# Two linear-attention and MLP layers in split precision: another order for the scaling, turning, norms, biases and last splits beside the MLP

## The chip, the cores and the metric

One core of a Trainium2 chip runs the whole program. The metric is device time in microseconds (us), the median of several runs. The core has five queues that work in order and side by side: TensorE (PE, with its weight loads as PEld), VectorE (DVE), ScalarE (ACT), GpSimd (POOL) and SyncE (SP), which here issues nearly all transfers between the core's memory and DRAM. An instruction that waits holds up all that is behind it in its own queue.

## The reference

x has 2048 tokens of 448 values; there are 16 heads of 28. Two layers, each

```
x = x + attention(layernorm(x))        # linear attention
x = x + gelu(layernorm(x) @ w1 + b1) @ w2 + b2      # 448 -> 1792 -> 448
```

with, for each head, phi(t) = where(t > 0, t + 1, exp(t)) + 1e-6:

```
kv  = sum_s phi(k_s) v_s^T ;  z = sum_s phi(k_s)
out = (phi(q) @ kv) / (phi(q) . z + 1e-6), joined over the heads, @ wo
```

Both layers use the same weights. LayerNorm has no scale or offset. All is float32.

## The kernel before

**Precision.** Each operand of a large matmul is split into a high part, which ACT makes by a cast to a rounded format, and a low part, the rest, which DVE (for weights POOL) makes by a subtraction. A product is then high by high, high by low and low by high, summed in PSUM. So every tile costs one ACT cast and one DVE subtraction before PE can use all of it.

**Stages of a layer.** The tokens are 16 tiles of 128 and four *groups* of four tiles (the code's b or k, 0 to 3); the 1792 inner values are 14 *chunks* of 128 (i, 0 to 13).

1. `phase1` (L797 on): for each tile LayerNorm, the K product, phi(K), and the sum G of x^T phi(K) over all tiles; Q products in between, phi(Q) to DRAM (`pq_d`).
2. A transition, written out token by token in `ORDER` (L733): G becomes the small matrix M (values, mask and wo in one, with parts `Mh`, `Ml`), and group 0 goes through attention. The rest of the Q products fills PE.
3. `classic` (L1326), twice: the MLP of group 0, then of group 1. Each step i issues the first product of the next chunk (`mlp1`, L1190: `hp`, 11 matmuls of 512 columns, then gelu and split), then `behind` (the attention of groups 1 to 3), then the second product (`mlp2`, L1210: `y`, 12 matmuls of 448 columns). In step 13 of group 0 the `mlp1` issued is the first of group 1.
4. `eight` (L1382), seven times: the MLP of groups 2 and 3 together, two chunks at a time by seven products (`hx`, `hy`, `hz`) of sums of inputs instead of eight.
5. `rest` (L1478): the second MLP product of group 3, with the beginning of the next layer in between, by the list `REST` (L1476).

**Turning.** PE needs inputs with the inner dimension on the partitions. For most tiles that is done without PE: DVE turns blocks of 32x32 (`turn`, L313, into tiles `sq`), SP stores the squares to DRAM (`store_sq`, L320) and loads them back rearranged (`spread`, L325, into tiles `sp`), and ACT and DVE split what came (`split_t`, L354: cast at L364, subtraction at L365). Two tiles share one 512 KB store and load.

**The list around the change.** `PLAN` (L1253) has one string for each of the 28 steps of the two `classic` passes, here called chunks 0 to 27; 0 to 13 lie beside group 0. `behind` issues its tokens in order, loads (tokens that begin with l) first. A token is a name, a group and a tile:

- `ld`: load phi(Q); `z` (L943): POOL multiplies it by the key sums; `p` (`q_prep`, L1064): DVE sums that to denominators, scales (L962 to L973) and turns; `sq`, `lq`: store and load of the squares (second digit: pair of tiles); `q`: the split into `qh`, `ql`.
- `o`: the attention product `op` on PE (`oc_mm`, L1014), then `o_ln` (L1027): DVE adds it to x (L1033), ACT forms mean and square sum, POOL the root `brs` (L1038), and SP stores x to DRAM (`r_d`).
- `n` (`m_prep`, L1072): ACT normalises (L1054), DVE turns; `sx`, `lx`: store and load; `x` (L351): the split into the MLP's input, `XH` and `XL`.
- `g`: load x; `r`: load x from `r_d`; `b` (L1057): POOL adds the bias of the MLP's output; `s`, `t`: the sums of inputs for `eight` (POOL and DVE) and their splits.

All four tiles of a group must have gone through `x` before the group's first `hp`. Weights for coming chunks are split in steps of a generator (`make`, L484; for `eight` the longer `sevens`, L445) by ACT, POOL and DVE.

Of the kernel before, what the change touches and what calls it, by code (L numbers as in the profile page):

```python
# [22 lines left out]
def linear_attn_mlp_kernel(  # L23
# [13 lines left out]
    x0 = x_in[0]  # L37
# [4 lines left out]
    NT = S // 128  # L42
# [667 lines left out]
    def stage_g(l, t, acc, mid=lambda: None):  # L710
# [21 lines left out]

    ORDER = [  # L733
# [3 lines left out]
    ] * LAYERS  # L737
    DEFER = NT - sum(tok in ("Q", "Qa", "Qy") for tok in ORDER[0].split())
# [58 lines left out]
    def phase1(l, tr):  # L797
        za = consts.tile([128, D], F32, name="za", tag="za")
        acc = []
        load_to(l, 4 if l == 0 else NORM[l][1][-1])  # L800
        if l == 0:
            launch(za)
            load_to(l, NORM[l][2][-1])
        for t in range(l == 0, NT):
            norm = NORM[l][t] if t < len(NORM[l]) else ()
            for tok in STEPS.get((l, t), STEP).split():
                if tok[1:].isdigit() and tok[0] in "anv":
                    {"a": stage_a, "n": stage_n, "v": stage_t}[tok[0]](l, int(tok[1:]))
                elif tok == "q1":
                    stage_qphi(1)  # L810
                elif tok == "sp":
                    for key, h in list(stored):
                        block(key)
                        spread(key, h)
                elif tok == "ld" and t + 2 < len(NORM[l]):
                    load_to(l, NORM[l][t + 2][-1])
                elif tok == "a":
                    for u in norm:
                        stage_a(l, u)
                elif tok == "n":  # L820
                    for u in norm:
                        stage_n(l, u)
                elif tok == "tu":
                    for u in norm:
                        stage_t(l, u)
                elif tok == "T" and t + 1 < NT:
                    stage_b(l, t + 1, "acc" if t == 1 else "h")
                elif tok == "X" and t + 1 < NT and (l == 0 or t >= 1):
                    stage_x(l, t + 1)
                elif tok == "K":  # L830
                    stage_k(l, t)
                elif tok == "qp":
                    stage_qphi()
                elif tok == "kp":
                    stage_kphi(l, t)
                elif tok == "kh":
                    stage_kh(l, t)
                    if l == 0:
                        begin(BG[t])
                elif tok == "kl":  # L840
                    stage_kl(l, t, za)
                elif tok == "s":
                    stage_s(l, t)
                elif tok == "G" and t >= 1:
                    acc = acc or [bank("acc", 4, f"G{c}")[:, :D] for c in range(4)]
                    stage_g(l, t - 1, acc)
                elif tok == "bg" and l == 0:
                    background(BG[t - 1])
                elif tok == "Q" and t < DEFER:
                    stage_q(l, t)  # L850
            if t == 12:
                tr.wv = stage_square(wqkv[:, 2 * D:])
            if t == 13:
                trans_load(l, tr)
        return za, acc
# [354 lines left out]
    def mlp2(l, b, i, then=lambda: None):  # L1210
# [46 lines left out]
        "p13 sq11 z20 g10 ld22",  # L1257
        "q10 lq11 p20 z21 g11 ld23",
        "q11 o10 p21 sq20 z22 g12",
        "q12 o11 n10 p22 z23 g13 ld30",  # L1260
        "q13 o12 n11 sx10 ld31",
        "o13 n12 lq20 p23 sq21 z30 ld32",
        "n13 lx10 sx11 p30 z31 g20 ld33",
        "x10 lq21 p31 sq30 z32",
        "lx11 q20 x11 p32 z33 g21",
        "q21 x12 x13 o20 g22",
        "q22 o21 n20 lq30 g23",
        "q23 o22 p33 n21 sq31 sx20 g30",
        "q30 o23 n22 g31",
        "q31 lq31 o30 n23 sx21 g32",  # L1270
        "q32 o31 n30 g33",
        "q33 o32 n31 sx30 lx21 r10",
        "o33 n32 lx20 tA111 r11",
        "n33 sx31 lx30 tA121 r12 b10",
        "lx31 tA110 r13 b11",
        "sS10 sS11 tA120 b12",
        "tS10 tS11 sS30 sS20 b13",
        "sS40 tS20 sS31 sS21",
        "tS21 sS41",
        "tS40 tS41",  # L1280
# [45 lines left out]
    def classic(l, b, tr):  # L1326

        if b == 0:
            mlp1(l, 0, 0)
            moves = trans_chunks(tr)  # L1330
        for i in range(NF):
            if i + 1 < NF:
                mlp1(l, b, i + 1)
            elif b == 0:
                mlp1(l, 1, 0)
            if b == 0:
                next(moves, None)
            n = first_pair(l, b) + i // 2 + 2
            late = b and i >= NF - 4
            if late:  # L1340
                make(first_pair(l, 2))
            elif i % 2:
                make(n)
            if i % 2 == 0 and (b == 0 or i < NF - 2):
                make(n + 1)
            behind(l, b * NF + i, tr)
            if b == 0 and 9 <= i < 13:
                add_bias(l, 0, i - 9)
            if b == 0 or i < NF - 2:
                mlp2(l, b, i)  # L1350
            if b == 0:
                next(moves, None)
            if late:
                make(first_pair(l, 2))
            elif i % 2 == 0:
                make(n)
            if b and i == NF - 1:
                make(n)

    def beside(l, k):  # L1360
# [21 lines left out]
    def eight(l, k):  # L1382

        n = first_pair(l, 2) + k
        c = Pair(l, k, n)
        onward = k == NP - 1 and l + 1 < LAYERS

        def step():
            if k < NP - 1:
                make(n + 1)  # L1390

        c.product(1)
        s1 = c.keep(c.X, "s1")
        if k:
            step()
            c.product(5)
            s5 = c.keep(c.Y, "s5")
            step()
            if onward:
                stage_a(l + 1, 0)  # L1400
            c.product(2)
            dve.tensor_tensor(s1, s1, c.Z, op=OP.add)
            c.high(s1, 0)
            step()
            c.product(6)
            s2 = c.keep(c.X, "s2")
            make(n)
            if k < NP - 2:
                make(n + 2)
            step()  # L1410
            mlp2(l, 2, 2 * k - 1)
            c.low(0)
            step()
            c.product(3)
            dve.tensor_tensor(s2, s2, c.Y, op=OP.add)  # L1415
            c.high(s2, 1)
            step()
            c.product(7)
            dve.tensor_tensor(s5, c.X, s5, op=OP.add)
            c.low(1)  # L1420
            c.later(s5, 1)
            step()
            beside(l, k)
            if onward:
                stage_a(l + 1, 1)
        else:
            mlp2(l, 1, NF - 2)
            c.product(2)
            dve.tensor_tensor(s1, s1, c.Z, op=OP.add)
            token_piece(l, "A22", 0)  # L1430
            c.high(s1, 0)
            make(n + 2)
            step()
            c.product(5)
            s5 = c.keep(c.Y, "s5")
            step()
            c.product(6)
            s2 = c.keep(c.X, "s2")
            c.low(0)
            mlp2(l, 1, NF - 1)  # L1440
            step()
            c.product(7)
            dve.tensor_tensor(s5, c.X, s5, op=OP.add)
            c.later(s5, 1)
            token_piece(l, "A22", 1)
            make(n)
            step()
            c.product(3)
            dve.tensor_tensor(s2, s2, c.Y, op=OP.add)
            c.high(s2, 1)  # L1450
            c.low(1)
            step()
        mlp2(l, 2, 2 * k)
        c.product(4)
        c.later(c.X, 0)
        step()
        if k == 0:
            step()
# [14 lines left out]

    gb = Came()

    REST = ("", "n0", "n1", "a2 m0", "s0 n2", "a3 m1", "n3", "p0 m0", "s1 a4 m0", "n4", "m1", "p1 x0", "x1 m1", "")  # L1476

    def rest(l):  # L1478

# [61 lines left out]
    for l in range(LAYERS):  # L1541
# [11 lines left out]
        def ahead_pq(j):  # L1553
# [12 lines left out]
            tq=lambda j: q_transpose(l, 0, j), qh=lambda j: q_high(l, 0, j), ql=lambda j: q_low(l, 0, j), o=lambda j: o_mm(l, 0, j, tr),  # L1566
            la=lambda j: o_ln(l, 0, j), lb=lambda j: o_n(l, 0, j), x=lambda j: m_part(l, 0, j), tu=lambda j: turn_xm(l, j),
            st=lambda j: store_sq(("m", l, 0), j), sp=lambda j: spread(("m", l, 0), j),
            sa=lambda j: spread(("m", l, 0), j), pl=ahead_pq, pre=lambda j: make(first_pair(l, 0) + 2), b=biases)
        for tok in ORDER[l].split():  # L1570
            name, j = tok.rstrip("0123456789"), int("0" + tok.lstrip("abcdefghijklmnopqrstuvwxyzQTG"))
            getattr(tok_, name)(j)
        assert not fill and not qo
        table(AF.Gelu_apprx_tanh)
        q_z(l, 1, 0, tr)
        for b in range(2):
            classic(l, b, tr)
        for k in range(NP):
# [30 lines left out]
```

## Time and profile before

| | us |
|---|---|
| median of three runs | 860.82 (860.04 to 862.4) |
| the profiled execution | 860.47 |
| its span, first to last instruction | 858.8 |
| PE busy | 847.9 (99%) |
| DVE, ACT, POOL busy | 576.5, 507.2, 388.6 |

The profile is of one execution. Its timeline gives start and duration of each instruction, by engine, source line and tile, and in brackets how long the engine stood idle before it and for whose result; where an x-count is above 1, neighbours alike are merged. The view of waits sums the same idle times by who waited for whom: us in total, times, longest. The windows view gives busy time of PE, PEld, DVE, ACT and POOL in a stretch, each with its count, then the granted TensorE clock as a share of full speed, the share of busy DMA time and GB/s. The chain of waits is the work that ended last, followed back in time. The source view of one line gives shortest, median and longest duration in ns.

### The profile page before, as it was taken

The page shows a single profiled execution, that of the slowest core. Times are in us where ns is not written, and L with a number is a line of the kernel's source. Part 1 is how long each engine was busy: PE and PEld are TensorE (multiplying, and loading weights), DVE is VectorE, ACT ScalarE, POOL GpSimd, SP SyncE. Part 2 cuts the span into 40 slices and gives each one's busy share as a digit, 9 for nine tenths or more (in the row PEclk, how much of TensorE's full clock was granted, in tenths as well). Part 3 has the DMA queues.
Part 4 walks back from the last instruction along what each step waited for, and adds up shares of the span by engine and source line. Part 5 has one row for each costly group of instructions (what it writes and reads, how often), then busy time and mean ns, then how long its engine had stood idle before and what let it go on. Part 6 is the DMA issues. An engine that isn't in the chain of part 4 may idle for free.

```text
span 858.8 us, 12486 instructions
## 1 busy us (share of the span) xinstructions
PE 847.9 (99%) x4085; PEld 755.5 (88%) x4085; DVE 576.5 (67%) x1022; ACT 507.2 (59%) x1051; POOL 388.6 (45%) x460
## 2 busy tenths in 40 slices
PE   9999999999999999999999999999999999999998
PEld 8899988887888888889989998988878888888897
DVE  7899597858643765456779976867776358545443
ACT  7667665465677576664446665555656766666531
POOL 3456524537335844750533343134563357454320
PEclk9999999999999999999999999999999999999999
DMA  5375746757567134437644543477576560333261
GB/s 172 121 249 178 241 138 197 244 180 251 181 208 236 35 119 126 142 96 245 219 151 160 181 141 118 142 229 241 161 241 221 189 197 25 105 109 98 91 233 44
DMA packets 103637, 142.92 MB, mean 166 GB/s; under 512 B 9876, under 2 KB 90644, under 8 KB 103572
## 3 DMA queue, kind: packets, MB, share of 16 engines
q1 hardware_dynamic: 101156, 138.77, 49.4%
q10 hardware_dynamic: 2416, 3.36, 1.2%
q8 instruction: 32, 0.52, 0.3%
q14 instruction: 33, 0.27, 0.1%
HBM read 88.94 MB, written 49.02 MB: 161 GB/s over the span
## 4 chain that ended last, share of the span: by engine, by line
PE 78%; DVE 9%; ACT 5%; issue 4%; POOL 2%; DMA 2%; SPq 0%; DVEq 0%; POOLq 0%; ACTq 0%
PE hp L1205 12%; PE y L1236 8%; PE y L1235 8%; PE y L1237 8%; PE hx L1147 8%; PE G L724 7%; PE psk L382 6%; PE psq L382 5%; PE hy L1147 4%; PE hz L1147 2%; DMA sp<-sq_m 1%; PE op L1023 1%; PE op L1022 1%; PE op L1021 1%; DVE pq L973 1%
## 5 line engine op out<-in xcount | busy, mean ns | idle before, releaser
L1236 PE MATMUL y<-w2l,gh 128*128 128x448 f32 x447 | 164.1, 367 | 0.0
L1235 PE MATMUL y<-w2h,gh 128*128 128x448 f32 x447 | 162.5, 364 | 0.1
L1237 PE MATMUL y<-w2h,gl 128*128 128x448 f32 x447 | 160.8, 360 | 0.0
L1205 PE MATMUL hp<-XH,W 128*128 128x512 f32 x392 | 123.4, 389 | 0.0
L1182 DVE TENSOR_TENSOR gl<-g,gh 128x512 fp32r<-128x512 f32 x84 | 69.2, 823 | 71.9 <-ACT gh L1178 71.7
L1235 PEld LDWEIGHTS y<-w2h,gh 128*128 128x128 f32 x447 | 83.9, 188 | 9.8 <-DVE x L1240 0.4
L1236 PEld LDWEIGHTS y<-w2l,gh 128*128 128x128 f32 x447 | 84.0, 188 | 6.8
L1237 PEld LDWEIGHTS y<-w2h,gl 128*128 128x128 f32 x447 | 84.0, 188 | 5.4
L1205 PE MATMUL hp<-XL,W 128*128 128x512 f32 x224 | 85.5, 390 | 1.6 <-DVE XL L365 1.6
L1205 PEld LDWEIGHTS hp<-XH,W 128*128 128x128 f32 x392 | 73.5, 188 | 12.9 <-ACT XH L364 0.3
L1159 ACT ACTIVATE g<-s,b1s 128x256 f32<-128x256 f32 x84 | 38.2, 502 | 55.0 <-DVE s L1415 34.9
L1038 POOL TENSOR_TENSOR brs<-bst,few 128x1 f32<-128x1 f32 x32 | 18.0, 564 | 105.6 <-ACT bst L1036 94.4
L1207 ACT ACTIVATE g<-hp,b1s 128x512 f32<-128x512 f32 x56 | 38.4, 685 | 42.5 <-PE hp L1205 39.9
L382 PE MATMUL psk<-wk,XH 128*128 128x448 f32 x210 | 61.8, 364 | 0.0
L563 POOL TENSOR_TENSOR xnl<-x,xnh 128x384 fp32r<-128x384 f32 x32 | 35.0, 1093 | 53.6 <-ACT xnh L562 30.6
L382 PE MATMUL psq<-wq,XH 128*128 128x448 f32 x196 | 57.2, 366 | 0.3 <-DVE eq L401 0.3
L425 POOL TENSOR_TENSOR W<-temp,W 128x256 fp32r<-128x256 f32 x56 | 48.1, 879 | 20.5 <-ACT W L424 20.5
L309 DVE STREAM_TRANSPOSE sq<-xm 128x384 f32<-128x384 f32 x32 | 20.7, 647 | 50.1 <-ACT xm L1054 49.9
L1178 ACT CAST gh<-g 128x512 fp32r<-128x512 f32 x84 | 52.2, 621 | 2.7
L1205 PEld LDWEIGHTS hp<-XL,W 128*128 128x128 f32 x224 | 41.9, 188 | 11.1 <-DVE XL L365 2.4
L951 POOL TENSOR_TENSOR pz<-pq,zb 128x448 f32<-128x448 f32 x24 | 29.1, 1214 | 45.8 <-DVE dn L962 45.8
L213 POOL TENSOR_TENSOR brs<-bve,few 128x1 f32<-128x1 f32 x31 | 17.1, 551 | 69.1 <-DVE bve L212 63.6
(252 smaller groups left out, 2162.1 us busy)
## 6 DMA issues: line engine op xcount, KB each, us to landing
temp<-in_B_w_dram SPq DMA_DIRECT2D x28, 384.0 KB
x<-in_A_x_dram SPq DMA_DIRECT2D x32, 224.0 KB
pq_d<-eq SPq DMA_DIRECT2D x32, 224.0 KB
pq<-pq_d SPq DMA_DIRECT2D x32, 224.0 KB
g_d<-g SPq DMA_DIRECT2D x28, 256.0 KB
x<-x_d SPq DMA_DIRECT2D x32, 224.0 KB
gb<-g_d SPq DMA_DIRECT2D x28, 256.0 KB
sq_a<-sq SPq DMA_DIRECT2D x13, 512.0 KB
```

What stands on the lines that cost most here:

```text
L382: pe.matmul(o, x, p, start=(i == 0), stop=(i == 10))
L425: pool.tensor_tensor(lo, x, f(hi), op=OP.subtract)
L724: pe.matmul(acc[c], w, k, start=first and c not in others[0], stop=last and c not in others[1])
L1147: pe.matmul(o, w, r, start=(k in (1, 5, 2) and i == 0), stop=(i == len(made) - 1), skip_group_check=True)
L1159: act.activation(g[:, s].rearrange("p (u i n) -> p i u n", u=2, i=4), x[:, s].rearrange("p (i u n) -> p i u n", u=2, i=4), AF.Gelu_apprx_t ...
L1178: act.copy(gh, g)
L1182: dve.tensor_sub(gl, g, f(gh))
L1205: pe.matmul(hp, w, r, start=(k == 0), stop=(k == len(made) - 1))
L1207: act.activation(g, hp, AF.Gelu_apprx_tanh, bias=b1s[:, i:i + 1])
L1235: pe.matmul(acc[j], gh[:, s], hi, start=first, stop=False)
L1236: pe.matmul(acc[j], gh[:, s], lo, start=False, stop=False)
L1237: pe.matmul(acc[j], gl[:, s], hi, start=False, stop=stop)
```

## The change

In `PLAN`:

- Norms `n` of groups 1 to 3 stand ahead of the next tile's sum `o` instead of behind it (chunks 6 to 8 and 13 to 19).
- `x10` goes from chunk 10 to chunk 11, behind `q20`. `p32` and `z33` go from chunk 11 to chunk 12, behind `x12 x13 o20`. The store `sq30` goes from chunk 10 to chunk 11, where the load `lx11` is issued ahead of it.
- The loads `r10` to `r13` go from chunks 18 to 21 to chunks 17 and 18, and the biases `b10` to `b13` from chunks 20 to 23 to 19 to 22.

In `classic`: the four biases of group 0 go from steps 9 to 12 to steps 5 to 8; the weight step that stood at the end of group 1's last step is issued in `eight` instead, behind the first product and its copy `s1`. In `ORDER`: `z10` is issued by a new token `z1` behind the third tile's statistics, instead of at the end of the list. At the seam of the layers: the splits x2 and x3 of layer 1's first group are done in the last step of `rest` instead of in `phase1`, with the store s1 a step earlier and the load p1 a step earlier (chunk 10 instead of 11).

```diff
-        "ms2 m3 ms3 ql0 Qy Qi tq2 qh2 pl1 pl0 pl2 qs3 o1 la1 ql2 o0 tq3 qh3 Qj Qs la0 lb1 ql3 tu1 st1 o2 la2 lb0 tu0 st0 sp1 o3 la3 lb2 tu2 st2 sp0 "
+        "ms2 m3 ms3 ql0 Qy Qi tq2 qh2 pl1 pl0 pl2 qs3 o1 la1 ql2 o0 tq3 qh3 Qj Qs la0 lb1 ql3 tu1 st1 o2 la2 lb0 z1 tu0 st0 sp1 o3 la3 lb2 tu2 st2 sp0 "
...
-                elif tok == "X" and t + 1 < NT and (l == 0 or t >= 1):
+                elif tok == "X" and t + 1 < NT and (l == 0 or t >= 3):
                     stage_x(l, t + 1)
...
         "q11 o10 p21 sq20 z22 g12",
-        "q12 o11 n10 p22 z23 g13 ld30",
-        "q13 o12 n11 sx10 ld31",
-        "o13 n12 lq20 p23 sq21 z30 ld32",
+        "q12 n10 o11 p22 z23 g13 ld30",
+        "q13 n11 o12 sx10 ld31",
+        "n12 o13 lq20 p23 sq21 z30 ld32",
         "n13 lx10 sx11 p30 z31 g20 ld33",
-        "x10 lq21 p31 sq30 z32",
-        "lx11 q20 x11 p32 z33 g21",
-        "q21 x12 x13 o20 g22",
-        "q22 o21 n20 lq30 g23",
-        "q23 o22 p33 n21 sq31 sx20 g30",
-        "q30 o23 n22 g31",
-        "q31 lq31 o30 n23 sx21 g32",
-        "q32 o31 n30 g33",
-        "q33 o32 n31 sx30 lx21 r10",
-        "o33 n32 lx20 tA111 r11",
-        "n33 sx31 lx30 tA121 r12 b10",
-        "lx31 tA110 r13 b11",
-        "sS10 sS11 tA120 b12",
-        "tS10 tS11 sS30 sS20 b13",
+        "lq21 p31 z32",
+        "lx11 q20 x10 x11 sq30 g21",
+        "q21 x12 x13 o20 p32 z33 g22",
+        "q22 n20 o21 lq30 g23",
+        "q23 n21 o22 p33 sq31 sx20 g30",
+        "q30 n22 o23 g31",
+        "q31 lq31 n23 o30 sx21 g32",
+        "q32 n30 o31 g33 r10 r11",
+        "q33 n31 o32 sx30 lx21 r12 r13",
+        "n32 o33 lx20 tA111 b10",
+        "n33 sx31 lx30 tA121 b11",
+        "lx31 tA110 b12",
+        "sS10 sS11 tA120 b13",
+        "tS10 tS11 sS30 sS20",
...
-            if b == 0 and 9 <= i < 13:
-                add_bias(l, 0, i - 9)
+            if b == 0 and 5 <= i < 9:
+                add_bias(l, 0, i - 5)
...
-            if b and i == NF - 1:
-                make(n)
...
         else:
+            step()
             mlp2(l, 1, NF - 2)
...
-    REST = ("", "n0", "n1", "a2 m0", "s0 n2", "a3 m1", "n3", "p0 m0", "s1 a4 m0", "n4", "m1", "p1 x0", "x1 m1", "")
+    REST = ("", "n0", "n1", "a2 m0", "s0 n2", "a3 m1", "n3", "p0 m0 s1", "a4 m0", "n4", "p1 m1", "x0", "x1 m1", "x2 x3")
...
-        q_z(l, 1, 0, tr)
         for b in range(2):
             classic(l, b, tr)
```

More of the change, by code (lines that the diff above doesn't have):

```diff
@@ L1568, in linear_attn_mlp_kernel @@
             st=lambda j: store_sq(("m", l, 0), j), sp=lambda j: spread(("m", l, 0), j),
-            sa=lambda j: spread(("m", l, 0), j), pl=ahead_pq, pre=lambda j: make(first_pair(l, 0) + 2), b=biases)
+            sa=lambda j: spread(("m", l, 0), j), pl=ahead_pq, z=lambda j: q_z(l, j, 0, tr), pre=lambda j: make(first_pair(l, 0) + 2), b=biases)
         for tok in ORDER[l].split():
```

## The prediction

> **What bounds the kernel now.** I read the page first, then TensorE's waits, then the timeline of TensorE at each wait, and last the other engines' timelines around those places.
>
> ```profile
> span 858.8 us, 12486 instructions
> PE 847.9 (99%) x4085; PEld 755.5 (88%) x4085; DVE 576.5 (67%) x1022; ACT 507.2 (59%) x1051; POOL 388.6 (45%) x460
> ```
>
> TensorE (PE) is the bound. The change removes no matmul, so it can gain only what PE loses in standing and restarting. What it stands for:
>
> ```profile
> PE op L1023 <- DVE ql L365: 3.1, 2, 2.0
> PE hp L1205 <- DVE XL L365: 1.6, 2, 0.9
> ```
>
> ```profile
> PEld hx L1147 <- ACT s L1151: 2.2, 4, 0.5
> ```
>
> Two waits at the attention product `op` (3.1 us), two at the first MLP product `hp` (1.6 us), four small ones in the seven-product stage. A gap costs more than its length. Undisturbed, matmuls follow each other in these steps:
>
> ```profile
> 40.72 2.21 PE psk L382 x11
> ...
> 215.82 2.49 PE hp L1205 x11
> ```
>
> ```profile
> L1205 PE MATMUL hp<-XH,W 128*128 128x512 f32 x392 | 123.4, 389 | 0.0
> ```
>
> The chain has a start every 2.21/11 = 0.20 us for 448 columns and every 0.226 us for 512, while the page has 0.389 us for one of 512: neighbours overlap by 0.16 us, and a gap loses that overlap too. The largest wait shows a second loss:
>
> ```profile
> 207.41 0.37 PE L1022 MATMUL op<-wq,qh 128*128 128x448 f32 x1
> 209.76 0.59 PE L1023 MATMUL op<-wq,ql 128*128 128x448 f32 x1 [1.98 <-DVE ql L365]
> ...
> 213.13 0.48 PE L1235 MATMUL y<-w2h,gh 128*128 128x448 f32 x1
> ```
>
> ```profile
> 209.76:213.13 3.37, 3.37 (x9) 2.99 (x10) 3.23 (x6) 0.10 (x1) 3.28 (x4) 0.53 0.83 268
> 631.88:633.80 1.92, 1.92 (x9) 1.80 (x10) 1.85 (x4) 0.40 (x1) 1.83 (x3) 1.00 0.96 313
> ```
>
> In the windows view the column before the DMA share is the granted clock. After the 1.98 us gap of layer 0 nine matmuls take 3.37 us instead of 9 x 0.20 = 1.80, at clock 0.53; after the same wait in layer 1 the clock stayed 1.00. So layer 0's wait costs 209.76 - 207.41 - 0.20 = 2.15 plus 3.37 - 1.80 = 1.57, together 3.72 us. The Trainium skill ("TensorE: Matmul & The Clock Gate", Part 1: The HAM clock gate) gives an idle window of about 3.4 us before the clock halves, so by it this 2 us gap would lose no clock. The trace shows that it did; by that page alone the gain here would be 2.15 and the forecast 1.6 us later.
>
> The other gaps:
>
> ```profile
> 136.10 0.50 PE L1205 MATMUL hp<-XL,W 128*128 128x512 f32 x1 [0.69 <-DVE XL L365]
> ...
> 446.85 0.47 PE L724 MATMUL G<-kl,xnh 128*128 128x448 f32 x1 [0.19 <-DVE kl L611]
> ...
> 631.88 0.47 PE L1023 MATMUL op<-wq,ql 128*128 128x448 f32 x1 [1.10 <-DVE ql L365]
> 638.88 0.50 PE L1205 MATMUL hp<-XL,W 128*128 128x512 f32 x1 [0.91 <-DVE XL L365]
> ```
>
> With the 0.16 us of overlap, and 0.11 us by which the restarted matmul is longer (0.50 against 0.39), they cost 0.96, about 0.4, 1.37 and 1.18 us.
>
> **The change part by part.**
>
> *x10 behind q20, p32 behind x13, the store sq30 behind the load lx11 (chunks 10 to 12, both layers).* This is the main term. VectorE (DVE) ahead of layer 0's wait:
>
> ```profile
> 200.90 0.64 DVE L1182 TENSOR_TENSOR gl<-g,gh 128x512 fp32r<-128x512 f32 x1
> 203.37 0.69 DVE L365 TENSOR_TENSOR XL<-sp,XH 128x512 fp32r<-128x512 f32 x1 [1.83 <-ACT XH L364]
> ...
> 207.15 0.36 DVE L310 STREAM_TRANSPOSE sq<-pq 128x128 f32<-128x128 f32 x1
> ...
> 208.49 1.21 DVE L365 TENSOR_TENSOR ql<-sp,qh 128x512 fp32r<-128x512 f32 x1
> ...
> 625.49 0.69 DVE L365 TENSOR_TENSOR XL<-sp,XH 128x512 fp32r<-128x512 f32 x1 [0.94 <-ACT XH L364]
> ```
>
> ```profile
> 202.71 0.62 ACT L364 CAST XH<-sp 128x512 fp32r<-128x512 f32 x1 [3.74 <-DMA sp<-sq_m]
> ...
> 213.03 1.14 ACT L364 CAST XH<-sp 128x512 fp32r<-128x512 f32 x2 [3.76 <-DMA sp<-sq_m]
> ```
>
> The row at 203.37 is x10, the LayerNorm split of tile 0 of group 1. DVE stands 1.83 us for it, because ScalarE (ACT) in turn waits for a spread (the load of turned squares) to land; p31 (204.0 to 207.5) and q20's low part `ql` (until 209.70), which PE needs, queue behind. Nobody needs x10 before the first MLP product of group 1, two chunks on. With x10 moved, p31 starts at 201.54 instead of 203.98, and `ql` ends 2.44 us earlier, near 207.3; PE asks for it with its third matmul, at 207.41 + 0.20 = 207.6. The margin is thin, but `ql` itself took 1.21 us here against 0.69 for the like split at 203.37, and ACT also loses x10's cast and wait. So the wait of layer 0 goes: 3.72 us. Layer 1 needs 1.10 us and gets 0.94 us of standing (its x10 is the row at 625.49) plus a split of 0.69: 1.37 us.
>
> Next late is the end of the same splits. In the chain these products begin at 215.82; without the stop they begin at about 212.1. PE needs all four high parts then, and the low parts after seven matmuls of 0.226, at 213.7. x12 and x13 come from lx11:
>
> ```profile
> 201.01 1.81 SPq L332 DMA_DIRECT2D sp<-sq_q  x1
> 207.53 0.34 SPq L323 DMA_DIRECT2D sq_q<-sq  x1
> 207.97 0.38 SPq L332 DMA_DIRECT2D sp<-sq_m  x1
> ```
>
> The queue SP stood from 202.82 to 207.53 for the store sq30, whose data p31 finishes on DVE at 207.51; only then could lx11 go, and it landed 5.06 us later (207.97 to 213.03). The new list puts the load ahead of that store, so it can go at about 203 (if its own store has landed, which no row shows), landing near 208 to 209: ACT's two casts (1.14) end near 210.2, DVE's two splits (0.69 each) near 212. So the margins are near 1.8 us, and p32 (3.5 us like p31) no longer stands ahead of x12 and x13. The layer 1 wait at 638.88 is this place: 1.18 us gone.
>
> *z10's early issue (token z1) at the head of the MLP.* The gap at 136.10 comes of this:
>
> ```profile
> 131.62 1.62 POOL L951 TENSOR_TENSOR pz<-pq,zb 128x448 f32<-128x448 f32 x1
> ```
>
> ```profile
> 131.01 2.77 DVE L365 TENSOR_TENSOR XL<-sp,XH 128x512 fp32r<-128x512 f32 x2
> ...
> 134.77 1.28 DVE L365 TENSOR_TENSOR XL<-sp,XH 128x512 fp32r<-128x512 f32 x2
> ```
>
> Two splits beside GpSimd's (POOL's) product take 2.77 us, two without it 1.28. With the product issued earlier, behind the third tile's statistics, DVE gets up to 1.49 us back and the gap of 0.69 goes: 0.96 us. There it stands on POOL ahead of the fourth tile's `brs`, which must wait for ACT's sums anyway; if that cover fails, x3 comes up to 1.62 us late and the gap returns (bounds: 0.96 gained, 0.7 lost).
>
> The same rivalry shows over all such splits, 0.67 to 1.65 us:
>
> ```profile
> L365 DVE TENSOR_TENSOR XL<-sp,XH x42: 668/700/1654, 45.9 to 638.1; 128x512 fp32r<-128x512 f32 x42
> ```
>
> *Biases at chunks 5 to 8 instead of 9 to 12.*
>
> ```profile
> L1059 POOL TENSOR_TENSOR x<-x,b2b 128x448 f32<-128x448 f32 x8 | 11.5, 1443 | 0.0
> ```
>
> ```profile
> 190.67 0.55 POOL L1038 TENSOR_TENSOR brs<-bst,few 128x1 f32<-128x1 f32 x1 [4.81 <-ACT bst L1036]
> ```
>
> Eight of 1.44 us. In one of their new chunks POOL stands 4.81 us ahead of a `brs` (the statistics' root that a norm needs), so I take the 1.44 us as covered: nothing; without the cover the `brs` behind is 1.44 us late per chunk. In the old chunks their going can only shorten DVE's 1.2 us splits.
>
> *Norms ahead of sums (n10 to n33).* The norm moves in front of the next tile's sum on ACT and DVE. It then needs statistics one chunk old only. What it stands for today:
>
> ```profile
> DVE sq L309 <- ACT xm L1054: 49.9, 20, 2.7
> ```
>
> Twenty times the turn waits up to 2.7 us for ACT's norm, which stood behind the tile's sums. Now the next tile's sum `x<-op`, and the scaling behind it, queue behind the turn on DVE, at most those 2.7 us late, while ACT's norm starts earlier by about as much. PE waits at none of these places today, so I cost it at nothing (bounds: the slower rival, and nothing); spreads go out earlier, which helps lx10 and lx11. The loads r10 to r13 and b10 to b13 a chunk earlier go with it on SP and POOL.
>
> *The last bias b13 out of chunk 23 and one weight step behind the first product.* This concerns the four small waits.
>
> ```profile
> 289.69 1.61 POOL L1059 TENSOR_TENSOR r<-r,b2b 128x448 f32<-128x448 f32 x1
> ```
>
> ```profile
> 298.37 0.62 ACT L464 CAST W<-raw 128x512 fp32r<-128x512 f32 x1 [3.57 <-POOL raw L460]
> ...
> 303.16 0.57 ACT L1151 COPY s<-hx 128x512 f32<-128x512 f32 x1
> ```
>
> PE waits for the copy `s`. ACT stood 3.57 us for POOL, which had b13 (1.61) in front, and one of the weight casts that ACT did just before now comes behind the copy. The copy comes up to 1.6 us earlier by the bias alone, and the first wait of each layer goes. The second hangs on DVE too; I take half. The bounds are nothing and all four, 2.2 us; 3/4 of 2.2 is 1.65, and since a weight load leads its matmul PE itself loses less: I take 1.25 us.
>
> *The splits x2 and x3 of layer 1 at the end of layer 0's rest.*
>
> ```profile
> 431.13 2.52 DVE L1240 TENSOR_TENSOR r<-y,r 128x448 f32<-128x448 f32 x4
> 436.41 0.63 DVE L401 SCALAR_TENSOR_TENSOR psk<-psk,ek 128x448 f32<-128x448 f32 x1 [2.76 <-ACT ek L399]
> ...
> 443.31 0.67 DVE L365 TENSOR_TENSOR XL<-sp,XH 128x512 fp32r<-128x512 f32 x1
> ```
>
> The split at 443.31 leaves the queue ahead of `kl`, whose wait at 446.85 is 0.19: about 0.4 us gained. In exchange the four sums at 431.13, their stores on SP and the loads of the next tiles behind come later by two splits, 1.3 to 3.3 us. Bounds: 0.4 gained to 3.3 lost; I take 0.4, since DVE stands 2.76 us behind the sums anyway.
>
> The sum is 3.72 + 1.37 + 1.18 + 0.96 + 1.25 + 0.4 = 8.9 us. The profiled execution took 860.47 us (span 858.8 and 1.67 around it), so 851.6; the median of the runs is 860.82, 0.35 above it, so I forecast a median of **851.9**.
>
> **The rivals.** *Exchange.* The stop moves from `op` to group 1's first `hp`, because lx11 goes no earlier than before (its own store not landed at 203, or the queue behind lq21's 1.81 us issue). If it lands at 213.03 as today, PE, there at 212.1, waits for the casts until 214.2: 2.1 us and a slow restart of 1.6, so layer 0 gains nothing; in layer 1 the boundary's 1.18 stays. That leaves 8.9 - 3.7 - 1.2 = 4.0: about 856.8. For it: the load is 512 KB behind another. Against it: SP plainly stood for sq30. Chance 0.15.
>
> *No change.* DVE is as late at 201.54 as before through the new norms and `ql` stays the last thing PE waits for; only the small places gain, 0.96 + 0.4, less new gaps of the same size: 859.5 to 861. Chance 0.06.
>
> *Slower: POOL against DVE.*
>
> The four biases now lie in chunks 5 to 8 beside the scaling and turning of p21 to p23 and before the four `brs`. If each pushes DVE by its full 1.44 us, DVE is 5.8 us later at p31; less the 2.44 us (layer 0) and 1.63 us (layer 1) won by x10, `ql` ends 3.4 and 4.2 us later than before, and layer 1 gets a slow restart (1.6) too: 9.2 us lost against 0.96 + 0.4 + 1.25 + 1.18 gained: 860.8 + 9.2 - 3.8 = about 866. It decides once DVE ends the `gl` of 200.90 later than about 204. Against it: POOL's long stands there, and that equal biases leave chunks 9 to 12. Chance 0.06. The Trainium skill ("SBUF — State Buffer", SBUF: two separate sides) says that the port pair which the two share is locked for a whole instruction and that the loser blocks fully; the 0.98 us between shortest and longest split agrees with part of such a block, not with 1.44.
>
> **How the numbers follow.** Forecast 0.70, exchange 0.15, no change 0.06, slower 0.06, else (half-way between forecast and exchange) 0.03. A measurement of this kernel tells about 0.3%, 2.6 us, from no change. Faster than 858.2: 0.70 + 0.15 + 0.03 = 0.88; within: 0.06; slower: 0.06. The forecast's own range is 850.5 (every priced wait gone and the unpriced remainder of 10.9 us of PE idle nearly so) to 854; to hold 8 in 10 with half of the exchange it reaches to 856.5.
>
> **What would show it.** Right: no PE wait on `ql` in either layer, no clock of 0.53, DVE going from `gl` straight to p31, the sq30 store after the lx11 load on SP, and PE busy within 3 us of its span. Wrong: a PE wait on `XH` or `XL` at group 1's first `hp` (exchange); a `gl` late in chunk 10 with long `brs` waits (slower); a new DVE stand after 433 for a tile of x that was loaded late.

## The result and the profile after

The changed kernel takes 850.73 us (median of four runs, 850.44 to 850.88) against 861.28 for the kernel before on the same chip (four runs, 860.04 to 862.4): 10.55 us less, ratio 0.9877 with a 95% interval of 0.986 to 0.9895. The forecast was 851.9, with a range of 850.5 to 856.5.

The page of the kernel after:

```profile
span 848.9 us, 12473 instructions
PE 842.9 (99%) x4085; PEld 754.8 (89%) x4085; DVE 574.2 (68%) x1022; ACT 510.4 (60%) x1051; POOL 386.4 (46%) x460
```

TensorE's waits, the whole list:

```profile
PE warm L171 <- DVE one L165: 1.1, 1, 1.1
PE psk L652 <- ACT wk L138: 0.8, 1, 0.8
PE psq L382 <- DVE eq L401: 0.3, 1, 0.3
```

All three lie in the start of the program and in phase 1 of layer 0. The waits at `op`, at `hp`, at the copy `s` and at G are gone. I also summed, over neighbouring matmuls, the time from start to start above the median for the shape of the first of the two (without the first 10 us of the program and without steps less than 0.05 us above it): 12.5 us before, 2.6 after. The difference, 9.9 us, is that of the two profiled executions (860.47 and 850.62). With 2.6 us left, little more is to be had from the order.

VectorE and TensorE in chunks 10 to 13 of layer 0:

```profile
199.69 0.66 DVE L1182 TENSOR_TENSOR gl<-g,gh 128x512 fp32r<-128x512 f32 x1
200.26 0.62 DVE L962 TENSOR_REDUCE dn<-pz 128x16 f32<-128x448 f32 x1
...
204.46 1.14 DVE L365 TENSOR_TENSOR ql<-sp,qh 128x512 fp32r<-128x512 f32 x1
205.52 1.82 DVE L365 TENSOR_TENSOR XL<-sp,XH 128x512 fp32r<-128x512 f32 x2
...
209.52 1.29 DVE L365 TENSOR_TENSOR XL<-sp,XH 128x512 fp32r<-128x512 f32 x2
```

```profile
207.14 0.36 PE L1023 MATMUL op<-wq,ql 128*128 128x448 f32 x1
...
211.35 0.62 PE L1205 MATMUL hp<-XH,W 128*128 128x512 f32 x2
```

VectorE goes from `gl` straight to p31 (the reduction at 200.26). q20's `ql` ends at 204.46 + 1.14 = 205.60, and PE uses it at 207.14: 1.5 us of margin where 2 us were missing. The last low parts of group 1 end at 210.81, ahead of its first `hp`. Note that `gl`, ahead of p31, also ran 1.2 us earlier than before (199.69 against 200.90). Moving x10, which is behind it, can't do that.

The queue SP at the same time:

```profile
196.29 0.32 SPq L323 DMA_DIRECT2D sq_m<-sq  x1
...
200.02 0.37 SPq L332 DMA_DIRECT2D sp<-sq_m  x1
203.84 0.33 SPq L323 DMA_DIRECT2D sq_q<-sq  x1
```

The load lx11 goes at 200.02, 7.95 us earlier than before, and the store sq30 behind it. Its own store, sx11 (196.29), also went 1.7 us earlier than before (198.01, quoted with the third experiment).

VectorE's waits for the norm, to be held against 49.9 us before:

```profile
DVE sq L309 <- ACT xm L1054: 11.5, 21, 1.2
```

The head of the MLP, POOL and then VectorE:

```profile
122.92 0.55 POOL L1038 TENSOR_TENSOR brs<-bst,few 128x1 f32<-128x1 f32 x1 [2.07 <-ACT bst L1036]
123.44 1.15 POOL L951 TENSOR_TENSOR pz<-pq,zb 128x448 f32<-128x448 f32 x1
125.38 0.55 POOL L1038 TENSOR_TENSOR brs<-bst,few 128x1 f32<-128x1 f32 x1 [0.79 <-ACT bst L1036]
```

```profile
131.52 1.79 DVE L365 TENSOR_TENSOR XL<-sp,XH 128x512 fp32r<-128x512 f32 x2
```

z10's product lies in a stand of POOL: the fourth tile's `brs` behind it still waits 0.79 us for ACT. The two splits that took 2.77 us beside it take 1.79.

### The profile page after: what moved, and what is told of

It reads as the page before. It is cut to its first block, busy times and chain, and to the rows that moved or that the text cites. A ratio compares the mean times of both kernels' runs of the same rounds, so it can differ in the third digit from the quotient of the medians.

```text
span 848.9 us, 12473 instructions
## 1 busy us (share of the span) xinstructions
PE 842.9 (99%) x4085; PEld 754.8 (89%) x4085; DVE 574.2 (68%) x1022; ACT 510.4 (60%) x1051; POOL 386.4 (46%) x460
## 4 chain that ended last, share of the span: by engine, by line
PE 96%; DVE 2%; DMA 1%; POOL 1%; issue 0%; ACT 0%; SPq 0%; DVEq 0%; POOLq 0%; ACTq 0%
PE hp L1205 16%; PE y L1236 11%; PE y L1235 11%; PE y L1237 10%; PE hx L1147 9%; PE G L724 7%; PE psk L382 7%; PE psq L382 7%; PE hy L1147 4%; PE hz L1147 2%; PE op L1022 2%; PE op L1021 2%; PE op L1023 2%; PE op L1011 1%; PE op L1010 1%; PE op L1012 1%
## 5 line engine op out<-in xcount | busy, mean ns | idle before, releaser
L724 PE MATMUL G<-kh,xnh 128*128 128x448 f32 x128 | 46.6, 367 | 0.0
L724 PE MATMUL G<-kl,xnh 128*128 128x448 f32 x128 | 46.1, 366 | 0.0
```

The costliest lines, as they stand in the source:

```text
L724: pe.matmul(acc[c], w, k, start=first and c not in others[0], stop=last and c not in others[1])
```

## The experiments

Three questions: what made the two large waits go, what the small edits are worth, and what a gap of PE costs. **My theory**, as predicted: x10's stand made `ql` late, and moving it, with lx11 ahead of sq30, is the gain; the norms are worth nothing. **The rival**: the norms ahead of the sums free VectorE and send the stores and loads out earlier, and that is the gain.

### x10 alone

The kernel before, with x10 behind q20; sq30 stays ahead of lx11.

```diff
-        "x10 lq21 p31 sq30 z32",
-        "lx11 q20 x11 p32 z33 g21",
+        "lq21 p31 sq30 z32",
+        "lx11 q20 x10 x11 p32 z33 g21",
```

> Before, with x10 alone moved from chunk 10 to chunk 11, behind q20. Theory 1 (x10's stand on DVE made ql late): both PE waits on ql go (3.7 + 1.4 us), but group 1's first hp now waits for x12 and x13, which still have p32 and a late lx11 ahead of them: about 1 us lost there per layer, so about 4 us faster than before, near 857. Theory 2 (the norms ahead of the sums made all of chunks 6 to 10 earlier, and that freed ql): at least half of the waits on ql stays, within 1.5 us of before.

Measured: 859.34 us (ten runs, 857.25 to 862.03) against 860.18; ratio 0.9995 (0.9981 to 1.0009). No change. TensorE, SP and ACT:

```profile
214.23 1.88 PE L1205 MATMUL hp<-XH,W 128*128 128x512 f32 x7 [2.06 <-ACT XH L364]
...
635.10 1.90 PE L1205 MATMUL hp<-XH,W 128*128 128x512 f32 x7 [2.15 <-ACT XH L364]
```

```profile
205.23 0.34 SPq L323 DMA_DIRECT2D sq_q<-sq  x1
205.67 0.38 SPq L332 DMA_DIRECT2D sp<-sq_m  x1
```

```profile
213.04 1.14 ACT L364 CAST XH<-sp 128x512 fp32r<-128x512 f32 x2 [3.58 <-DMA sp<-sq_m]
```

Both waits for `ql` went, as my theory has it, and both came back one product later: group 1's `hp` waits for the casts of x12 and x13, whose load lx11 went at 205.67 behind sq30 and landed near 213. Of the 4 us that I expected nothing came, because I had put the loss at `hp` at about 1 us a layer and it is over 2. This is the rival "exchange" of the prediction, in both layers. A queue that stops less doesn't help if the next thing PE needs is no earlier.

lx11 even went 2.3 us earlier than before (205.67 against 207.97) and still landed no sooner (213.03 before). So the same load took 7.4 us instead of 5.06. From 204 to 208 us the windows view has the DMA engines at a share of 1.03 here, fully busy (350 GB/s), and before at 0.62 (212 GB/s). That the other transfers of these 4 us are the cause fits, but no run takes them away.

### Chunks 10 to 12 as in the change

The kernel before, with x10, the order of lx11 and sq30, and p32 and z33 as in the change; the norms stay behind the sums.

```diff
-        "x10 lq21 p31 sq30 z32",
-        "lx11 q20 x11 p32 z33 g21",
-        "q21 x12 x13 o20 g22",
+        "lq21 p31 z32",
+        "lx11 q20 x10 x11 sq30 g21",
+        "q21 x12 x13 o20 p32 z33 g22",
```

> Before, with the edits of chunks 10 to 12 alone: x10 behind q20, the store sq30 behind the load lx11, p32 and z33 behind o20. Theory 1: waits on ql and on XL at group 1's first hp all go, 6.3 us (3.7 + 1.4 + 1.2) faster than before, near 855. Theory 2: at most 3 us faster.

Measured: 854.92 us (854.28 to 856.6), ratio 0.9947 (0.9929 to 0.9965): 5.3 us less by the medians, where my theory had 6.3 and the rival at most 3. What is left at these places, in TensorE's waits, in SP's timeline and in SP's waits:

```profile
PE hp L1205 <- ACT XH L364: 0.8, 1, 0.8
```

```profile
200.97 1.53 SPq L332 DMA_DIRECT2D sp<-sq_q  x1
204.25 0.37 SPq L332 DMA_DIRECT2D sp<-sq_m  x1
```

```profile
SPq L332 <- DMA sq_m<-sq: 1.7, 1, 1.7
```

lx11 is ahead of sq30 now, but still leaves only at 204.25, 4.2 us later than in the changed kernel: it waits for its own store to land. It lands 7.25 us later, near 211.5, where ACT's cast ends a wait of 2.30 us for it, and start to start 0.94 us is lost at `hp` in layer 0. In layer 1 no wait is left there.

### The norms alone

The kernel before, with the ten norms n10 to n33 ahead of the sums and nothing else; for group 1:

```diff
-        "q12 o11 n10 p22 z23 g13 ld30",
-        "q13 o12 n11 sx10 ld31",
-        "o13 n12 lq20 p23 sq21 z30 ld32",
+        "q12 n10 o11 p22 z23 g13 ld30",
+        "q13 n11 o12 sx10 ld31",
+        "n12 o13 lq20 p23 sq21 z30 ld32",
```

> Before, with the norms of groups 1 to 3 ahead of the next tile's sum, and nothing else. Theory 1: x10 still stands ahead of ql, at most 1 us faster. Theory 2: both waits on ql go, 5 us faster.

Measured: 854.27 us (854.05 to 854.72), ratio 0.9937 (0.9922 to 0.9952): 5.9 us less, where the prediction had nothing. VectorE's waits, VectorE's timeline and TensorE's waits:

```profile
DVE sq L309 <- ACT xm L1054: 13.5, 20, 1.2
```

```profile
200.40 0.68 DVE L365 TENSOR_TENSOR XL<-sp,XH 128x512 fp32r<-128x512 f32 x1
201.01 0.61 DVE L962 TENSOR_REDUCE dn<-pz 128x16 f32<-128x448 f32 x1
```

```profile
PE hp L1205 <- DVE XL L365: 1.6, 3, 0.7
```

Loads and stores of group 1's norms on SP, first before, then with the norms ahead:

```profile
196.93 0.37 SPq L332 DMA_DIRECT2D sp<-sq_m  x1
...
198.01 0.44 SPq L323 DMA_DIRECT2D sq_m<-sq  x1
```

```profile
193.03 0.37 SPq L332 DMA_DIRECT2D sp<-sq_m  x1
...
196.49 0.32 SPq L323 DMA_DIRECT2D sq_m<-sq  x1
```

x10 still stands where it stood, ahead of p31, but nobody waits for it: its load lx10 went at 193.03 instead of 196.93, its data is there, and the row at 200.40 has no bracket. So p31 starts at 201.01 instead of 203.98, and no wait for `ql` is left. So VectorE's stand of 1.83 us goes in either of two ways: x10 moves behind, or its data comes in time, as here. What is left is 0.62 us, start to start, at group 1's `hp` in each layer (the third of the three waits is the gap near 136).

### The changed kernel without the norms

The changed kernel, with all ten norms back behind the sums; for group 1:

```diff
-        "q12 n10 o11 p22 z23 g13 ld30",
-        "q13 n11 o12 sx10 ld31",
-        "n12 o13 lq20 p23 sq21 z30 ld32",
+        "q12 o11 n10 p22 z23 g13 ld30",
+        "q13 o12 n11 sx10 ld31",
+        "o13 n12 lq20 p23 sq21 z30 ld32",
```

> After, with the norms back behind the sums. Theory 1: nothing comes back but some margin is lost, at most 1 us slower than after (851 to 852). Theory 2: the waits on ql come back, 4 to 5 us slower than after.

Measured: 853.13 us (852.29 to 854.38), ratio to the kernel before 0.992 (0.9902 to 0.9938), so 2.4 us slower than the changed kernel by the medians. The two were measured on different chips; held against the kernel before on its own chip, it gains 7.05 us where the changed kernel gains 10.55, 3.5 us less. TensorE's waits, then the one of layer 0, VectorE and SP:

```profile
PE hp L1205 <- ACT XH L364: 3.0, 2, 1.9
PE y L1237 <- DVE gl L1182: 0.2, 1, 0.2
```

```profile
213.62 1.65 PE L1205 MATMUL hp<-XH,W 128*128 128x512 f32 x6 [1.94 <-ACT XH L364]
```

```profile
213.08 1.29 DVE L365 TENSOR_TENSOR XL<-sp,XH 128x512 fp32r<-128x512 f32 x2 [3.06 <-ACT XH L364]
```

```profile
204.89 0.37 SPq L332 DMA_DIRECT2D sp<-sq_m  x1
```

It lies between the two expectations (at most 1, and 4 to 5), and the waits for `ql` that the rival expected did not come back. The waits are at `hp` again, in both layers, because lx11 leaves at 204.89. They are longer than with chunks 10 to 12 alone (1.94 us here in layer 0, 0.8 there), and a wait of 0.2 us for `gl` is new. The two kernels differ in the small edits, group 0's biases among them; which of these does it, no run isolates.

### Group 1's norms alone, and both parts together

First the kernel before with n10 to n12 alone.

```diff
-        "q12 o11 n10 p22 z23 g13 ld30",
-        "q13 o12 n11 sx10 ld31",
-        "o13 n12 lq20 p23 sq21 z30 ld32",
+        "q12 n10 o11 p22 z23 g13 ld30",
+        "q13 n11 o12 sx10 ld31",
+        "n12 o13 lq20 p23 sq21 z30 ld32",
```

> The kernel before with the norms of group 1 alone (chunks 6 to 8) ahead of the sums. Theory (what the norms gain lies in VectorE's queue ahead of the two waits for ql, and only group 1's norms stand ahead of them): all of the gain of the experiment with all norms, 5 to 6 us faster than before, no wait of op for ql, at most 0.7 us at group 1's first hp in each layer. Rival (the earlier norms of groups 2 and 3 take part of it, because they start the loads and splits of the seven-product stage earlier): 3 us faster or less.

Measured: 855.58 us (855.25 to 856.21) against 859.85; ratio 0.995 (0.9936 to 0.9963), 4.3 us less, against 5.9 with all ten norms: between the theory (5 to 6) and the rival (3 or less). The trace has no wait for `ql` and 0.66 and 0.63 us lost at group 1's `hp`, as expected. The remaining 1.6 us are not settled: the intervals overlap (0.9936 to 0.9963 and 0.9922 to 0.9952), and the trace shows only about 0.2 us more in each layer, behind the next `op`.

Then the kernel before with all ten norms (those of groups 2 and 3 likewise) and chunks 10 to 12 as in the second experiment.

```diff
...
-        "x10 lq21 p31 sq30 z32",
-        "lx11 q20 x11 p32 z33 g21",
-        "q21 x12 x13 o20 g22",
+        "lq21 p31 z32",
+        "lx11 q20 x10 x11 sq30 g21",
+        "q21 x12 x13 o20 p32 z33 g22",
...
```

> The kernel before with the norms ahead of the sums and chunks 10 to 12 as in the change, and nothing else of it. Theory (the two parts free the same queue, so their gains overlap, and together they clear both places): 6.5 to 7.5 us faster than before, no wait for ql, XH or XL above 0.2 us at op or at group 1's first hp; the waits of 136, 303, 443 and 726 as before. Rival (the gains add up, 5.4 and 4.6): 10 us faster. Second rival (one of the two is enough): 5.5 us faster.

Measured: 853.33 us (853.23 to 853.47), ratio 0.9924 (0.9911 to 0.9938): 6.5 us less, where the parts alone gave 5.9 and 5.3. In TensorE's waits one line for `hp` is left, which is the gap near 136:

```profile
PE hp L1205 <- DVE XL L365: 0.7, 1, 0.7
```

So the two parts overlap: each frees the same stretch of VectorE's and SP's queues. The norms alone leave 0.62 us at `hp` in each layer, the chunks alone 0.94 in layer 0, and together they leave nothing. Either part alone gets most of it, and with overlapping intervals (0.9922 to 0.9952 and 0.9929 to 0.9965) the runs don't say which is worth more. The changed kernel with only chunks 10 to 12 as before was not run.

### Group 0's biases

The changed kernel, with the biases back at steps 9 to 12.

```diff
-            if b == 0 and 5 <= i < 9:
-                add_bias(l, 0, i - 5)
+            if b == 0 and 9 <= i < 13:
+                add_bias(l, 0, i - 9)
```

> The changed kernel with group 0's four biases back at steps 9 to 12. My theory (POOL stands in steps 5 to 8 anyway, and the biases were in nobody's way where they were): at most 0.5 us slower than the changed kernel, no wait of TensorE above 0.3 us at group 1's first product. The rival (the biases beside the splits of x10 to x13 and q20 are what makes these splits take 1.2 us instead of 0.69): four splits 0.5 us longer in each layer, so 1 to 2 us slower, with waits for XL or XH back at group 1's first product in both layers.

Measured: 850.22 us (849.63 to 850.43), ratio to before 0.9877 (0.9862 to 0.9891), the same as the changed kernel, and TensorE's waits are at the same three places at the start and nowhere else. In the changed kernel this move is worth nothing, as I expected; with the norms behind the sums it was not tried by itself.

### z10's early issue and the seam

The changed kernel with z10 at the end of the transition again, and with x2 and x3 of layer 1 in phase 1 again.

```diff
-        ... la2 lb0 z1 tu0 st0 ...
+        ... la2 lb0 tu0 st0 ...
...
-                elif tok == "X" and t + 1 < NT and (l == 0 or t >= 3):
+                elif tok == "X" and t + 1 < NT and (l == 0 or t >= 1):
...
-    REST = (..., "p1 m1", "x0", "x1 m1", "x2 x3")
+    REST = (..., "p1 m1", "x0", "x1 m1", "")
...
+        q_z(l, 1, 0, tr)
         for b in range(2):
```

> The changed kernel with z10 back at the end of the transition and with x2 and x3 of layer 1 back in phase 1: two places far apart, read separately in the trace. My theory: the gap near 136 comes back with its 0.96 us (two splits 2.77 us again beside POOL's product), the smaller one at the same place of layer 1 with about 0.3, and the one ahead of G near 443 with about 0.4 to 0.7: 1.7 to 2 us slower in all. The rival (those gaps went for another reason, because work around them starts earlier now): under 0.5 us slower and no TensorE wait above 0.3 us at these places.

Measured: 851.88 us (850.92 to 852.01), ratio 0.9895 (0.988 to 0.9909), 1.5 to 1.7 us slower than the two kernels on the same chip that lose nothing (850.43 with the weight step back, in the next section, and 850.22 with group 0's biases back). VectorE, then TensorE at both places:

```profile
131.52 2.76 DVE L365 TENSOR_TENSOR XL<-sp,XH 128x512 fp32r<-128x512 f32 x2
```

```profile
136.60 0.72 PE L1205 MATMUL hp<-XL,W 128*128 128x512 f32 x2 [0.68 <-DVE XL L365]
```

```profile
441.89 0.47 PE L724 MATMUL G<-kl,xnh 128*128 128x448 f32 x1 [0.19 <-DVE kl L611]
```

Measured start to start, 0.84 us come back at 136.60 (0.94 with the matmul behind it), 0.46 at 441.89 and about 0.2 at z10's place in layer 1. All three terms are near the forecast.

The one at 441.89 is less sure than it looks. The same wait of 0.19 us for `kl` also stands in three kernels that keep the new seam: the one without the norms and both of "A dose of gap" below. In those VectorE first stands for a tile of x that is loaded late; without the norms:

```profile
435.69 0.63 DVE L207 BATCH_NORM_STATS2 bst<-x 128x6 f32<-128x448 f32 x1 [0.34 <-DMA x<-x_d]
```

That is the price that the prediction named for the seam, later loads of the next tiles. The changed kernel has no such stand, so its 0.46 us hang on that load being in time.

### The weight step and the last bias

First the changed kernel with the weight step back at the end of group 1's last step.

```diff
+            if b and i == NF - 1:
+                make(n)
...
-            step()
             mlp2(l, 1, NF - 2)
```

> The changed kernel with the weight step back at the end of group 1's last step, the bias b13 left early. My theory (the bias and the step removed one each of the two waits for the copy s in each layer): one wait of each layer comes back, about 0.45 us each, 0.9 us slower. First rival (the bias alone removed both): under 0.2 us slower, no wait for s. Second rival (the step alone removed both): 1.7 us slower with two waits in each layer.

Measured: 850.43 us (850.21 to 850.6), ratio 0.988 (0.9863 to 0.9896). No wait for `s` is back. Then the changed kernel with r10 to r13 and b10 to b13 back a chunk later.

```diff
-        "q32 n30 o31 g33 r10 r11",
-        "q33 n31 o32 sx30 lx21 r12 r13",
-        "n32 o33 lx20 tA111 b10",
+        "q32 n30 o31 g33",
+        "q33 n31 o32 sx30 lx21 r10",
+        "n32 o33 lx20 tA111 r11",
...
-        "sS10 sS11 tA120 b13",
-        "tS10 tS11 sS30 sS20",
+        "sS10 sS11 tA120 b12",
+        "tS10 tS11 sS30 sS20 b13",
```

> The changed kernel with the loads r10 to r13 and the biases b10 to b13 back at their old chunks (b13 in chunk 23), the weight step left behind the first product. My theory (the bias and the step removed one each of the two waits for the copy s in each layer): the first wait of each layer comes back, about 0.45 us each, 0.9 us slower. First rival (the step alone removed both): under 0.2 us slower. Second rival (the bias alone did it): 1.7 us slower with two waits in each layer.

Measured: 852.5 us (851.6 to 853.06), ratio 0.9903 (0.9888 to 0.9918), 2.1 to 2.3 us slower than the two kernels named above (850.22 and 850.43). TensorE's waits, and the one of layer 0:

```profile
PE hx L1147 <- ACT s L1151: 1.2, 2, 0.6
```

```profile
303.95 0.74 PE L1147 MATMUL hx<-XH,W 128*128 128x512 f32 x2 [0.60 <-ACT s L1151]
```

My theory, one wait for each edit, failed in both runs. The rival that holds is that the bias alone removes both waits of each layer, the first of the step's run and the second of this one; the step alone removes nothing. With the step moved and the bias late there is one wait of 0.6 instead of two small ones, and start to start it costs 0.8 to 0.9 us a layer, as the two did before: 1.7 of the 2.1 to 2.3 us; the rest is not accounted for. ACT's timeline with the bias late, and then in the changed kernel:

```profile
294.30 0.62 ACT L464 CAST W<-raw 128x512 fp32r<-128x512 f32 x1 [3.57 <-POOL raw L460]
```

```profile
293.08 0.62 ACT L464 CAST W<-raw 128x512 fp32r<-128x512 f32 x1 [2.47 <-POOL raw L460]
```

With the bias late the cast waits 3.57 us for POOL, as in the kernel before, and without it 2.47. So POOL's lead reaches the copies through ACT's queue.

### A dose of gap

The changed kernel with q20's low split done four times, then nine times; the same result each time, on VectorE ahead of what PE waits for.

```diff
-        eng.tensor_tensor(lo.rearrange("p c (i n) -> p c i n", n=32), x, f(h), op=OP.subtract)
+        for _ in range(4 if key[0] == "q" and key[2] == 2 and t == 0 else 1):
+            eng.tensor_tensor(lo.rearrange("p c (i n) -> p c i n", n=32), x, f(h), op=OP.subtract)
```

> The changed kernel with the split of q20's low part done four times instead of once (the same result, three more VectorE instructions of 0.69 to 1.2 us ahead of what PE waits for, in each layer). In the changed kernel ql ends about 1.3 us before PE asks for it in layer 0, so three more make PE wait 0.8 to 2.2 us in each layer. If a gap costs its length and the lost overlap of 0.16: 2 to 5 us slower than the changed kernel, runs within 0.7 us of each other. If each gap near 2 us also halves the clock for the next nine matmuls: up to 3 us more, clock near 0.5 behind it in the profiled run. If only some do: runs spread by 1.6 to 3 us.

Measured: 852.35 us (851.9 to 852.86), ratio to before 0.9913 (0.9899 to 0.9926).

```profile
PE op L1024 <- DVE ql L366: 1.9, 2, 0.9
```

Each gap costs 1.10 us from start to start, 0.94 and the 0.16 of lost overlap, 2.2 in all, and the mean clock of all four runs is 1.00. So the gaps cost their length and the overlap, as the first case has it. The medians, from two chips, are 1.6 us apart, and the four runs lie within 0.96 us, where I expected 0.7.

> The changed kernel with the split of q20's low part done nine times: eight more VectorE instructions, at least 5.5 us, so PE waits 4 to 6 us in each layer. If a gap costs its length and 0.16: 8.5 to 12 us slower than the changed kernel. If a gap of this length always halves the clock for about 3.4 us behind it: 3 us more than the lengths in the trace, a clock near 0.5 behind both gaps, and runs within 0.7 us of each other, since it is no longer a matter of chance. If only some gaps do: runs spread by 1.6 to 3 us.

Measured: 863.27 us (862.78 to 863.32), ratio to before 1.0038 (1.0025 to 1.0051). TensorE at the first gap, and the windows behind both:

```profile
211.85 0.74 PE L1024 MATMUL op<-wq,ql 128*128 128x448 f32 x1 [4.57 <-DVE ql L366]
```

```profile
211.85:216.49 4.64, 4.64 (x12) 4.12 (x13) 4.43 (x9) 0.20 (x1) 0.00 (x0) 0.50 0.03 10
636.02:639.90 3.88, 3.88 (x11) 3.46 (x12) 3.88 (x7) 0.00 (x0) 0.00 (x0) 0.56 0.02 6
```

Behind both gaps of 4.6 us the clock is near half. By start-to-start times the first gap costs 4.7 + 2.3 and the second 4.7 + 1.7 us, and the five runs, with mean clocks of 0.994 to 0.996, lie within 0.54 us: at this length it was no matter of chance. The 4.0 us beyond the gaps are more than the 3 expected.

## Why the prediction was right, and where it wasn't

The sum was 8.9 us; the profiled executions differ by 9.85 (860.47 and 850.62) and the medians by 10.55. Sign, place and size were right. What the prediction had wrong is how the gain is shared out among the edits. By its steps:

- **`op` in both layers and group 1's `hp`** (3.72 + 1.37 + 1.18 = 6.3): cleared. The edits that the prediction names, chunks 10 to 12, are worth 5.3 us by themselves, and 6.5 with the norms. Within them one step failed: "With x10 moved, p31 starts at 201.54" is true (201.64 with x10 alone), but "So the wait of layer 0 goes: 3.72 us" is no gain of that move, which alone is worth nothing (859.34 against 860.18), since the stop goes to `hp`.
- **"I cost it at nothing"**, of the norms: the step that failed. They alone are worth 5.9 us. I had quoted the row that says so (49.9 us of VectorE's waits for ACT's norm) and dismissed it because PE waits at none of those twenty places. They lie on the path all the same: 36 of these 50 us went, and group 1's stores and loads went to SP earlier. "Spreads go out earlier, which helps lx10 and lx11" stood in half a sentence without a price. The sum came out nonetheless because the gains of norms and chunks overlap, so that leaving one of them out costs little; that is in part luck.
- **lx11 "can go at about 203 (if its own store has landed, which no row shows)", "landing near 208 to 209"**: without the norms neither held. The load left at 204.25 and 204.89 in the two runs with lx11 ahead of sq30 and the norms behind, and at 200.02 in the changed kernel. With chunks 10 to 12 alone it took 7.25 us to land instead of the 5.06 of the kernel before. So the change meets the condition through the norms, and the chance of the exchange, 0.15, had been read from SP's stand for sq30 alone.
- **z10** (0.96): 0.94, shown by taking it back. The 0.2 to 0.3 us of the same place in layer 1 had been left out.
- **The seven-product stage** (1.25 of 2.2): all four waits went, about 0.83 us a layer start to start, so 1.7. The half was taken off for a second cause, VectorE, and the step was named beside the bias; with the step at its old place nothing came back, so the early bias is enough.
- **The seam** (0.4): 0.46 came back with the old seam, but three kernels with the new seam lose it too.
- **Group 0's biases** (nothing): nothing in the changed kernel; the rival "POOL against DVE" didn't come near its point of decision there, since `gl` ends at 200.35 and not past 204.
- **The slow restart** (1.57 of the 3.72): a price that is paid in some runs, as the last section shows. The profiled execution had paid it. How many of the runs behind the median of 860.82 had, the record doesn't say.
- **"PE busy within 3 us of its span"**, a sign of being right, did not come: 848.9 less 842.9 is 6.0 us. In both kernels 1.1 us before the first matmul and 3.6 behind the last belong to it, and no edit here touches them. The other signs came.

## What to carry to other kernels

A wait of the bottleneck engine is worth tracing back not to the instruction that stands last, but through that to the first producer that is late for no need; here VectorE's stand of 1.8 us for a late load also goes when norms queued behind sums, some chunks earlier, move ahead. A long total of small waits on an engine that is not the bound is lateness for everything behind it in that queue, its stores and loads included, so it may not be costed at nothing because the bound engine doesn't wait at those places. And of a set of edits that free the same stretch, the gains don't add: each alone exchanges one wait for another or gets most of it.

## What the runs showed of the chip

A gap of TensorE costs its length, 0.16 us of overlap, and sometimes a slow restart, by the length of the gap. At 0.94 us (two gaps a run) there was none. At about 2 us it came and went: the kernel before had a clock of 0.53 for 3.37 us behind 1.98 us, while the kernel with x10 moved had two gaps of 2.06 and 2.15 us and none in its profiled execution, which is the quickest of its ten runs, and the changed kernel without the norms had none behind 1.94. Four of the ten runs with x10 moved, with a mean clock of 0.999 or 1.000, took 857.25 to 858.21 us; the six at 0.996 to 0.998 took 859.02 to 862.03. By an estimate from the trace of the kernel before, half a clock for 3.4 of 858 us lowers the mean by 0.002, so these six fit one or two slow restarts each. At 4.57 us it came behind both gaps, for 4.64 and 3.88 us.

The Trainium skill ("TensorE: Matmul & The Clock Gate", Part 1: The HAM clock gate) has the clock halved after an idle window of about 3.4 us. It calls that window free-running, and says that the same kernel therefore has a different number of slow matmuls from run to run. The gaps of 0.94 and 4.57 us agree with the threshold, and the mean clocks of the ten runs, which differ, agree with a window that runs free; the 1.98 us gap with a clock of 0.53 does not agree with the threshold, and the trace decides. What sets it for one gap of 2 us and not for another no run here shows.

On the same chip four runs of the kernel before lie between 860.04 and 862.4 us and four of the changed one between 850.44 and 850.88. That the removed gaps narrowed the spread is not shown: with chunks 10 to 12 alone no gap of the profile is longer than 1.1 us and the mean clock is 1.00 in all four runs, and yet these lie between 854.28 and 856.6 us.
